# Scores of the first step issued early, its neighbour's loads moved to SyncE, and weight passes one by one, in a gated linear recurrence followed by a PReLU network

## The chip, the cores and the metric

The kernel runs on one core of one Trainium2 chip. A core has TensorE (PE, matmuls), VectorE (DVE), ScalarE (ACT), GpSimd (POOL) and SyncE (SP); the last two mostly issue transfers here. The metric is the device time of one execution in microseconds (us). The kernel before takes 625.14 us, the median of three executions (624.67, 625.14, 626.03).

## The reference

Two parts follow one another. The first is a gated linear recurrence over 768 tokens, for 4 batches, 8 heads and a head dimension of 48:

```python
f = 1.0 / (1.0 + np.exp(-f_logit))
for t in range(S):
    state = f[:, :, t, :, None] * state + np.einsum('bhd,bhe->bhde', k[:, :, t], v[:, :, t])
    y[:, :, t] = np.einsum('bhd,bhde->bhe', q[:, :, t], state)
```

Its output, regrouped to 3072 tokens of 384 numbers, goes through a feed-forward network with 2048 hidden units and a PReLU with one alpha per unit:

```python
h = x @ w_in                                        # 384 -> 2048
g = np.maximum(h, 0.0) + alpha * np.minimum(h, 0.0)
return (g @ w_out).astype(np.float32)               # 2048 -> 384
```

Inputs and output are float32. The weights reach the chip as 64-bit words that hold float64 values, and the kernel turns them into float32 itself.

## The kernel before

**Steps.** The sequence is cut into 6 chunks of 128 tokens, the batches into 2 pairs. A step is one chunk of one batch pair; the 12 steps run in the order (pair 0, chunk 0), (pair 1, chunk 0), (pair 0, chunk 1) and so on. Tiles of a step carry the suffix `pair_chunk`, so step 0 is `0_0` and step 1 is `1_0`. Each step passes through four generators:

- `prepare` (key P, or Q for the step to come) loads f, q, k and two halves of v, takes the sigmoid of f on ScalarE (L267), copies q into `qd` (L270), and forms on VectorE the products of decays that the scores need: `qd` with its four lags (L275), running products by two scans (L305, L307), `us` (from ScalarE's copies at L302, multiplied at L309), `k4` (L335), `kh`, `ks`, `q3` and, for chunk 0 alone, 16-column pieces `k16` and `q16` (L375, L392). At its end ScalarE copies `q3` into the matrix `A` (L407).
- `carry` (key O) multiplies the off-diagonal 32x32 blocks `off` (L432) and, for chunk 0, the 16-column blocks (L442). ScalarE copies the latter into `ad` (L446) and the former into `A` (L450). For chunk 0 it transposes `ks` on TensorE (`pk`, L459) and copies it to `ksn` (L462). Then the state products `pd` (L472) update the state kept in `vs` (L482 to L488).
- `attend` (key S) computes, for each batch u of the pair, the scores inside groups of four tokens (`raw`, 32 small matmuls for each u, L508), which VectorE merges into `ad` by four masked copies (L514), and the scores between groups (`qu`, L523), merged by three masked copies in chunk 0 (L545) and seven in the others (L529). ScalarE then copies `ad` into the diagonal blocks of `A` (L551), TensorE multiplies `A` with the state and values (`py`, L562), ScalarE copies the result to `y` (L571), and `xT`, the network's input, is made from `y`: in step 0 by matmuls (`xt`, L580, copied at L582), in the other steps by transfers.
- `network` (key n) computes eight blocks `ph` of the hidden layer, six matmuls each (L606); for each, ScalarE forms the negated negative part (`neg`, L611) and VectorE the gate (L613). Step 0 then multiplies by `w_out` plainly (`po`, L626). The other steps use a seven-product scheme (`pa` to `pe`, L645) on sums `S` of the gates (L687) and on sums of halves of `w_out` (L706, key W), which VectorE forms once.

**Weights.** `load_weights` brings each of `w_in` and `w_out` in 8 pieces of 767 KB into tiles `raw` on SP's queue (L196; four buffers, so the first four are issued at the start). For each piece ScalarE makes three passes: `pos` (L201), `neg` (L203) and `low` (L204), the last straight into the weight tile and the last reader of the `raw` tile; VectorE then forms `lead` from pos and neg (L214) and adds it into the weight tile (`both`, L219). One `a` (w_in) or `b` (w_out) in the order runs all three passes of one piece; `w` and `v` run one lead and the both of the piece before.

**Order.** The order on TensorE, VectorE and ScalarE is written out by hand; the two issuing engines follow by dependences. For step n the string `first[n]` (n from 0 to 3) or `usual` is read key by key; each key runs a generator up to its next `yield`, a number repeats it. In body n, key P, O and S belong to step n, n to the network of step n - 1, and Q to `prepare` of step n + 1.

**PSUM.** Two tiles of two banks (`pair`) serve off, pk, pd, raw, qu and py; four single banks (`bank`) serve ph, xt, po, pa to pe. At the start 56 tiny matmuls into the bank `idle` (L733) run before any other work of TensorE.

**Who loads.** Step 0's f, q, k and v are issued by SP ahead of the weights; all later steps' by POOL (L250).

Of the kernel before, what the change touches and what calls it, by code (L numbers as in the profile page):

```python
# [18 lines left out]
DB = 32  # L19
# [7 lines left out]
IDLE = 56  # L27
RAWS, TOPS, LEADS = 4, 3, 4
# [3 lines left out]
def kernel(  # L32
# [135 lines left out]
    def load_weights(dst, src, name):  # L168
# [17 lines left out]
        got = {}  # L186
# [7 lines left out]
        def upper(n):  # L194
            raw = stage.tile([128, WP, 4], I16, tag="raw", name=f"{name}_raw{n}", bufs=RAWS)
# [3 lines left out]
            top = raw[:, :, 2]  # L199
            pos = stage.tile([128, WP], I16, tag="pos", name=f"{name}_pos{n}", bufs=TOPS)  # L200
            nc.scalar.activation(pos, top, AF.Relu, bias=bias[:, 0:1], scale=8.0)  # L201
            neg = stage.tile([128, WP], I16, tag="wneg", name=f"{name}_neg{n}", bufs=TOPS)
            nc.scalar.activation(neg, top.bitcast(U16), AF.Relu, bias=bias[:, 1:2], scale=8.0)  # L203
            nc.scalar.activation(as_int(n, I32), by_row(raw.bitcast(U32)[:, :, 0]), AF.Copy, scale=2.0 ** -13)  # L204
            got[n] = raw, pos, neg
# [5 lines left out]
        def lead(n):  # L211
            raw, pos, neg = got.pop(n)
# [7 lines left out]

        def uppers():
            for n in range(pieces_):
                upper(n)
                yield
# [9 lines left out]
        return uppers(), rests()  # L234
# [11 lines left out]
    def prepare(bp, c, x):  # L246
# [3 lines left out]
        loads = nc.gpsimd if bp or c else nc.sync  # L250
# [169 lines left out]
    def carry(bp, c, x):  # L420
# [3 lines left out]
        off = pair(f"off_{i}")  # L424
        for u in range(U):
            for hp in range(HP):
                for cc in range(NC2):
                    g = (u * HP + hp) * NC2 + cc
                    o = (u * HP + hp) * DB
                    for par in range(2):  # L430
                        r_ = rows(par)
                        nc.tensor.matmul(off[CH * cc:CH * cc + DB, par, o:o + DB],  # L432
                                         lhsT=kh[r_, g], rhs=q3[r_, g, 2], start=True, stop=True)
        if not c:
            for u in range(U):
                for hp in range(HP):
                    for j in range(NJ):
                        g = (u * HP + hp) * NJ + j
                        o = U * HP * DB + (u * HP + hp) * 16
                        for par in range(2):  # L440
                            r_ = rows(par)
                            nc.tensor.matmul(off[DB * j:DB * (j + 1), par, o:o + 16], lhsT=x["k16"][r_, g],  # L442
                                             rhs=x["q16"][r_, g], start=True, stop=True)
            for u in range(U):
                o = U * HP * DB + u * HP * 16
                nc.scalar.copy(ad[:, u, :, :, 16:DB], off[:, :, o:o + HP * 16].rearrange("p r (h t) -> p r h t", h=HP))  # L446
        for cc in range(NC2):
            s_ = slice(CH * cc, CH * cc + DB)
            for par in range(2):
                nc.scalar.copy(A[s_, :, par * HP:(par + 1) * HP, CH * cc + DB:CH * (cc + 1)],  # L450
                               off[s_, par, 0:U * HP * DB].rearrange("p (u h t) -> p u h t", u=U, h=HP))
# [347 lines left out]
```

## Time and profile before

| What | us |
|---|---|
| Median of three executions | 625.14 |
| The profiled execution, whole | 626.43 |
| Its span (first to last instruction) | 624.6 |
| TensorE busy in the span | 589.2 (94%) |
| VectorE busy | 503.4 (81%) |
| ScalarE busy | 260.5 (42%) |
| POOL busy | 62.9 (10%) |
| First `ph` matmul of step 0 | starts 57.88 |
| Step 1's `f` lands; its sigmoid starts | 24.0; 36.55 |
| Last add of the first seven-product network | ends 158.3 |

A profile is of one execution. "Busy" is the time in which an engine executed something; matmul ends are modelled, so a busy TensorE need not be at its best. In a timeline a line reads: start, duration of the group, engine, source line, operation, output<-input by tile names, shape, number of instructions (a float32 matmul of the kernel shows as two), and in brackets the idle time before it with the engine, tile and line that ended it. "PEclk" and "granted clock" are the share of TensorE's full clock that it was given. Line numbers are those of the kernel before.

### The profile page before, as it was taken

The page shows a single profiled execution, that of the slowest core. Times are in us where ns is not written, and L with a number is a line of the kernel's source. Part 1 is how long each engine was busy: PE and PEld are TensorE (multiplying, and loading weights), DVE is VectorE, ACT ScalarE, POOL GpSimd, SP SyncE. Part 2 cuts the span into 40 slices and gives each one's busy share as a digit, 9 for nine tenths or more (in the row PEclk, how much of TensorE's full clock was granted, in tenths as well). Part 3 has the DMA queues.
Part 4 walks back from the last instruction along what each step waited for, and adds up shares of the span by engine and source line. Part 5 has one row for each costly group of instructions (what it writes and reads, how often), then busy time and mean ns, then how long its engine had stood idle before and what let it go on. Part 6 is the DMA issues. An engine that isn't in the chain of part 4 may idle for free.

```text
span 624.6 us, 19118 instructions
## 1 busy us (share of the span) xinstructions
PE 589.2 (94%) x8220; PEld 525.9 (84%) x8220; DVE 503.4 (81%) x1013; ACT 260.5 (42%) x482; POOL 62.9 (10%) x119
## 2 busy tenths in 40 slices
PE   3457999999999999999999999999999999999997
PEld 3346876789889889889889889889889889889997
DVE  7589989899799798889889888888888889762261
ACT  5797992261443252342343343243244244223110
POOL 9120010001001001001001001001001000000000
PEclk9998999899999999999999999999999999999999
DMA  9866513213314313413413313413314301201000
GB/s 298 278 225 196 200 41 93 75 35 86 87 36 90 82 35 86 87 35 85 87 35 85 75 49 85 83 38 87 73 49 85 68 22 26 53 3 26 26 0 26
DMA packets 68116, 50.43 MB, mean 81 GB/s; under 512 B 47168, under 2 KB 60608, under 8 KB 68032
## 3 DMA queue, kind: packets, MB, share of 16 engines
q1 hardware_dynamic: 56656, 25.01, 15.8%
q0 software_dynamic: 6864, 22.35, 12.6%
q10 hardware_dynamic: 4512, 1.85, 1.6%
q8 instruction: 65, 1.06, 0.8%
q14 instruction: 19, 0.16, 0.1%
HBM read 36.21 MB, written 4.72 MB: 66 GB/s over the span
## 4 chain that ended last, share of the span: by engine, by line
PE 60%; DVE 18%; ACT 16%; issue 4%; DMA 1%; ACTq 1%; DVEq 0%
PE ph L606 24%; PE pc L645 9%; PE pa L645 6%; PE pe L645 5%; PE pd L645 5%; ACT A L551 4%; ACT us L302 3%; DVE gate L613 3%; PE qu L523 3%; DVE S L687 3%; PE raw L508 3%; DVE qd L275 2%; PE py L562 2%; ACT neg L611 2%; PE pb L645 1%
## 5 line engine op out<-in xcount | busy, mean ns | idle before, releaser
L606 PE MATMUL ph<-xT,w_in_sb 128*128 128x256 f32 x1152 | 262.7, 385 | 0.0
L606 PEld LDWEIGHTS ph<-xT,w_in_sb 128*128 128x128 f32 x1152 | 216.8, 191 | 33.1 <-issue 2.6
L611 ACT ACTIVATE neg<-ph 128x512 f32<-128x512 f32 x96 | 57.1, 596 | 197.2 <-PE ph L606 156.1
L613 DVE SCALAR_TENSOR_TENSOR gate<-neg,om,ph 128x256 f32<-128x256 f32 x192 | 82.2, 478 | 50.3 <-ACT neg L611 50.2
L645 PE MATMUL pc<-t,S 128*128 128x192 f32 x352 | 61.7, 329 | 0.0
L645 PE MATMUL pa<-w_out_sb,gate 128*128 128x192 f32 x352 | 61.0, 327 | 0.0
L645 PEld LDWEIGHTS pa<-w_out_sb,gate 128*128 128x128 f32 x352 | 58.0, 190 | 0.6
L645 PEld LDWEIGHTS pc<-t,S 128*128 128x128 f32 x352 | 57.3, 190 | 0.6
L514 DVE COPY_PREDICATED ad<-mraw,raw 128x256 f32<-128x256 int32 (+1 forms) x96 | 42.4, 441 | 8.3 <-PE raw L508 5.8
L529 DVE COPY_PREDICATED ad<-mquad,qu 128x224 f32<-128x224 int32 (+6 forms) x140 | 41.9, 300 | 6.2
L407 ACT COPY A<-q 48x512 f32<-48x512 f32 x44 | 27.2, 617 | 37.4 <-DVE q L356 37.0
L551 ACT COPY A<-ad 32x256 f32<-32x256 f32 x96 | 38.6, 402 | 1.4
L318 DVE TENSOR_TENSOR us<-us,fs 128x768 f32<-128x768 f32 (+5 forms) x60 | 36.7, 612 | 0.0
L663 ACT COPY o<-pa 128x192 f32<-128x192 f32 x11 | 3.5, 318 | 75.3 <-PE pa L645 72.3
L562 PEld LDWEIGHTS py<-A,vs 128*64 128x64 f32 x768 | 25.7, 145 | 7.8 <-ACT A L551 3.3
L562 PE MATMUL py<-A,vs 128*64 128x64 f32 x768 | 28.7, 232 | 3.4 <-ACT A L551 1.4
L687 DVE TENSOR_TENSOR S<-gate 128x512 f32<-128x512 f32 x44 | 30.3, 688 | 0.8
L645 PE MATMUL pb<-t,gate 128*128 128x192 f32 x176 | 30.4, 326 | 0.0
L645 PE MATMUL pe<-w_out_sb,S 128*128 128x192 f32 x176 | 30.4, 326 | 0.0
L645 PE MATMUL pd<-w_out_sb,S 128*128 128x192 f32 x176 | 30.4, 326 | 0.0
L508 PEld LDWEIGHTS raw<-qd,k 48*32 48x32 f32 x1536 | 18.3, 109 | 14.0 <-issue 8.4
L508 PE MATMUL raw<-qd,k 48*32 48x80 f32 x1536 | 23.3, 243 | 6.8 <-ACT A L450 5.2
(109 smaller groups left out, 754.6 us busy)
## 6 DMA issues: line engine op xcount, KB each, us to landing
w_out_raw<-in_w_out SPq DMA_DIRECT2D x8, 767.8 KB, 4.4
w_in_raw<-in_w_in SPq DMA_DIRECT2D x8, 767.2 KB, 9.8
q<-in_qT POOLq DMA_DIRECT2D x11, 512.0 KB, 4.4
f<-in_fT POOLq DMA_DIRECT2D x11, 512.0 KB, 4.2
k<-in_kT POOLq DMA_DIRECT2D x11, 512.0 KB, 4.6
out<-o SPq DMA_DIRECT2D x24, 192.0 KB, 2.8
vs<-in_v POOLq DMA_DIRECT2D x22, 192.0 KB, 4.6
ksn<-kt SPq DMA_DIRECT2D x80, 32.0 KB, 2.0
```

The costliest lines, as they stand in the source:

```text
L318: nc.vector.tensor_tensor(us[:, :, UO[m]:UO[m] + 4 * n].rearrange("p g (i r) -> p g i r", r=4), us[:, :, skip:skip + 4 * n].rearrange("p g ...
L407: nc.scalar.copy(A[halves(cc)[1], :, par * HP:(par + 1) * HP, CH * cc:CH * (cc + 1)], q3[rows(par)].rearrange("p (u h c) s t -> p u h c (s ...
L508: nc.tensor.matmul(raw[DB * j:DB * (j + 1), par, hp * C:hp * C + QW], lhsT=k[r_, g * DB:(g + 1) * DB], rhs=qd[r_, g], start=True, stop=True)
L514: nc.vector.copy_predicated(adu[:, :, :, d:4], mraw[:, d, :, d:4].bitcast(I32).unsqueeze(1).broadcast_to((128, H, NB, n)), rv[:, :, QO[d]: ...
L529: nc.vector.copy_predicated(ad[:, u, :, :, 4 * m:DB], mquad[:, lo:lo + n].bitcast(I32).unsqueeze(1).unsqueeze(1).broadcast_to((128, 2, HP, ...
L551: nc.scalar.copy(A[s_, u, :, s_], ad[s_, u].rearrange("p r h t -> p (r h) t"))
L562: nc.tensor.matmul(py[64 * par:64 * par + 64, u, o:o + CH], lhsT=vs[bp][:, cc, u, hd * D:hd * D + 64], rhs=A[:, u, par * HP + hp, CH * cc: ...
L606: nc.tensor.matmul(ph[:, j * T:(j + 1) * T], lhsT=w_in_sb[:, kt, m * 128:(m + 1) * 128], rhs=xT[:, kt], start=(kt == 0 and j == 0), stop=( ...
L611: nc.scalar.activation(neg, phv, AF.Relu, scale=-1.0)
L613: nc.vector.scalar_tensor_tensor(gate[:, m % NH, m // NH], neg[:, j], om[:, m:m + 1], phv[:, j], ALU.mult, ALU.add)
L645: nc.tensor.matmul(to[:, 0:DH], lhsT=of(f), rhs=by(f), start=(f == 0 and not more), stop=(f == NH - 1), skip_group_check=True)
L687: nc.vector.tensor_tensor(to, x_, y_, op)
```

## The change

Six things change together.

1. The 56 tiny matmuls at the start become 46, and a new key J runs single filler matmuls (128x256) into the bank `idle`, later into a bank `spare`: 15 in all, inside step 0.
2. In step 0, `attend` issues the raw scores of both batches right after `qd` is ready, ahead of `off`, then merges both and issues both quad-score groups, then merges those. Later steps keep their order inside `attend`.
3. In step 0, `off` and `pk` take single banks instead of a pair. In all chunk-0 steps the 16-column blocks come before the 32-column ones, and their copy into `ad` is four instructions instead of two; step 0 yields between `off` and `pk`.
4. f, q, k and v of step 1 are loaded by SP instead of POOL. On SP's queue they stand behind six pieces of w_in.
5. One `a` runs one pass of one piece (pos, neg or low); one generator covers w_in and then w_out. Three `raw` buffers instead of four; piece n + 3 is requested after low of piece n.
6. The four strings `first` are rewritten; `usual` stays. In body 1, six blocks `ph` of step 0's network stand on TensorE ahead of off, pk and raw of step 1; before, off and pk stood ahead of all of them and raw behind the first ones.

The diff, cut to its core:

```diff
-IDLE = 56
-RAWS, TOPS, LEADS = 4, 3, 4
+IDLE = 46
+RAWS, TOPS, LEADS = 3, 3, 4
...
-        def upper(n):
-            raw = stage.tile([128, WP, 4], I16, tag="raw", name=f"{name}_raw{n}", bufs=RAWS)
+        def fetch(n):
+            raw = raws[n] = stage.tile([128, WP, 4], I16, tag="raw", name=f"{name}_raw{n}", bufs=RAWS)
             nc.sync.dma_start(...)
+        def upper(n):
             pos = ...
             nc.scalar.activation(pos, top, AF.Relu, bias=bias[:, 0:1], scale=8.0)
+            yield
             neg = ...
             nc.scalar.activation(neg, top.bitcast(U16), AF.Relu, bias=bias[:, 1:2], scale=8.0)
-            nc.scalar.activation(as_int(n, I32), by_row(raw.bitcast(U32)[:, :, 0]), AF.Copy, scale=2.0 ** -13)
+            yield
+            low = raws.pop(n).bitcast(U32)[:, :, 0]
+            nc.scalar.activation(as_int(n, I32), by_row(low), AF.Copy, scale=2.0 ** -13)
...
-        loads = nc.gpsimd if bp or c else nc.sync
+        loads = nc.gpsimd if c else nc.sync
...
-        off = pair(f"off_{i}")
+        def two(name):
+            if plain:
+                return [bank(f"{name}{n}_{i}") for n in range(2)]
+            t = pair(f"{name}_{i}")
+            return [t[:, n] for n in range(2)]
+        off = two("off")
...
             for u in range(U):
-                o = U * HP * DB + u * HP * 16
-                nc.scalar.copy(ad[:, u, :, :, 16:DB], off[:, :, o:o + HP * 16].rearrange(...))
+                for par in range(2):
+                    o = U * HP * DB + u * HP * 16
+                    nc.scalar.copy(ad[:, u, par, :, 16:DB], off[par][:, o:o + HP * 16].rearrange(...))
...
+        if (bp, c) == steps[0]:
+            raws = [scores(u) for u in range(U)]
+            yield
+            qus = []
+            for u in range(U):
+                within(u, raws[u])
+                qus.append(quad_scores(u))
+            yield
+            for u in range(U):
+                between(u, qus[u])
+            yield
+        else:
+            for u in range(U):
+                within(u, scores(u))
+                between(u, quad_scores(u))
+                yield
...
+    def kept_busy():
+        while True:
+            if not spare:
+                spare.append(bank("spare"))
+            nc.tensor.matmul(spare[0][:, 0:256], lhsT=ones[:, 0:128], rhs=ones[:, 0:256], start=True, stop=True)
+            yield
...
-        "P5 a w P a2 O w S w a w a2 S Q S O S w Q2 S Q2 S w",
-        "a2 w b w O w n2 b2 v S P v2 n2 S b v Q n b n O S2 v n b v n Q2 b v Q b n S v2 W Q W S n2 W n W",
-        "n S P n2 S n W n O Q n3 O S Q n S Q n Q S2 Q n3",
-        "S n3 P S Q S n O n O n4 Q S Q S Q n S Q n Q n2",
+        "J4 P J P a2 P a J a S J2 a J a2 J w a P J a2 P J3 w J O P S2 Q w a w a S O S O Q S a Q S a2 Q a2 w Q w",
+        "a2 n a2 w a2 n2 a n a w a P v a n w n O a3 S a2 v a n a S v a v S a n a2 v O a Q a4 n S v a4 Q v n a S n S v2 Q2 W n Q W3",
+        "n S n P n3 S Q S n2 O n O n S W n Q3 S2 Q n Q n2",
+        "S n2 S2 n Q n O Q n S n2 O n2 Q2 n S Q n2 S Q n",
...
+    def uppers(parts):
+        for n in range(RAWS):
+            parts[n][0](parts[n][2])
+        for n, (_, upper, m) in enumerate(parts):
+            yield from upper(m)
+            if n + RAWS < len(parts):
+                fetch, _, ahead = parts[n + RAWS]
+                fetch(ahead)
+            yield
```

## The prediction

> **What bounds the kernel now.** I read the page's totals and 40 slices first, then the waits of VectorE, then the timelines of TensorE and ScalarE at the places that the change touches, and the DMA issues last.
>
> ```profile
> PE 589.2 (94%) x8220; PEld 525.9 (84%) x8220; DVE 503.4 (81%) x1013; ACT 260.5 (42%) x482; POOL 62.9 (10%) x119
> ...
> PE   3457999999999999999999999999999999999997
> ...
> DVE  7589989899799798889889888888888889762261
> ACT  5797992261443252342343343243244244223110
> ```
>
> TensorE is full from slice 5 on; the first four slices (62 us) are all that a start-up change can shorten. But VectorE is above nine tenths in many slices until the tenth as well. Its waits between 12 and 160 us, by what released it (total, times, longest):
>
> ```profile
> DVE ad L514 <- PE raw L508: 4.8, 1, 4.8
> DVE gate L613 <- ACT neg L611: 4.3, 4, 1.3
> DVE w_in_lead L214 <- ACT w_in_neg L203: 2.4, 1, 2.4
> DVE w_out_lead L214 <- ACT w_out_neg L203: 1.0, 1, 1.0
> DVE qd L275 <- ACT qd L270: 0.6, 1, 0.6
> DVE us L309 <- ACT us L302: 0.5, 1, 0.5
> ```
>
> That is 13.6 us, the last of it before 91 us; from there to the end of the first seven-product network (the L672 add, ending 158.3 us) VectorE waits for nobody. So up to 158 us I keep the account by VectorE: its instructions number 1013 in both kernels, and the handover to a full TensorE moves by the change in the sum of these waits. The lines that carry the steps, TensorE first:
>
> ```profile
> 27.93 1.34 PE L508 MATMUL raw<-qd,k 48*32 48x80 f32 x64 [5.21 <-ACT A L450]
> ...
> 46.97 2.83 PE L580 MATMUL xt<-y,dense 128*128 128x256 f32 x12 [1.79 <-ACT y L571]
> ...
> 57.88 4.40 PE L606 MATMUL ph<-xT,w_in_sb 128*128 128x256 f32 x18
> ```
> ```profile
> 118.17 1.07 PE L523 MATMUL qu<-us,k 48*32 48x112 f32 x64 [1.19 <-DVE ad L529]
> 119.17 7.40 PE L606 MATMUL ph<-xT,w_in_sb 128*128 128x256 f32 x24
> ```
> ```profile
> 36.55 1.04 ACT L267 ACTIVATE f<-f 128x1024 f32<-128x1024 f32 x1
> ...
> 43.47 2.14 ACT L302 COPY us<-qd 128x256 f32<-128x256 f32 x4
> ```
> ```profile
> w_in_raw<-in_w_in SPq DMA_DIRECT2D x8, 767.2 KB, 9.8
> ...
> f<-in_fT SPq DMA_DIRECT2D x1, 512.0 KB, 4.0
> ...
> f<-in_fT POOLq DMA_DIRECT2D x1, 512.0 KB, 8.7
> ```
>
> To see: step 0's raw scores wait for the off-diagonal block; its network starts at 57.9; after a wait of 1.2 us among small matmuls, 24 first-layer instructions (two blocks) took 7.40 us where the same 24 take 5.45 at 110.68 (granted clock 0.77 over that stretch); and step 1's sigmoid starts at 36.6 although its f landed at 24.0.
>
> **The change part by part.** The sum is made against the profiled execution, 626.43 us (span 624.6, 1.8 around it); the median shown, 625.14, lies 1.29 under it, so a difference found on the profile is added to 625.14.
>
> *Early scores.* qd is ready at 10.6; the raw matmuls of both batches (64 instructions and 1.34 each) now run there, to 13.3. Their merge (L514) can't follow at once: VectorE first does step 0's products, which end at 20.2, and one lead pass is put in front of them that waits for neg0 (15.2 instead of 14.7: +0.5 wait, 0.5 work that is done anyway). So products end near 20.8, a lead and a both (1.5) follow, and the merges start at 22 instead of 29.42, behind the L446 copies (off 16-wide matmuls 1.43, copies 0.7). Waits of 2.4 and 4.8 go; the second quad-score pair comes 0.5 late. Two merges with quads (2 x 2.9) end near 28.5 instead of 38.1. L446 grows from 2 copies (0.41 together) to 4 (about 0.7): +0.3 on ScalarE in a stretch where it waits for f next, hidden.
>
> *Weights pass by pass, three buffers, and the loads on SP.* ScalarE's 4.0 us wait before L407 goes; passes run from 13.34 at 0.89, 0.87 and 0.79 each, so low0, low1 and low2 end at 16.0, 18.6 and 21.2. They release raw3, raw4, raw5 on SP, in order, and only behind raw5 stand f, q, k and two vs of step 1. f is issued at 21.2 + 0.65 = 21.9 (POOL issued it at 15.26). Bounds of its landing: 4.0 after issue, the row of an f on SP with nothing in front (25.9), and 8.7, the row of the crowded f (30.6). In front of it stand raw4 and raw5 partly, 1.0 to 1.5 MB at 376 to 417 KB per us (the full slices of the DMA view up to 45 us) 2.5 to 4 us, so I take 5.5 in all: 27.4. ScalarE reaches the sigmoid near 25.3 and waits 2.1; nothing else is behind it that VectorE could use except neg3. q and k land by about 31; q (ready about 29) is needed after kr at 29.1. POOL loses four of its DMA issues (2.8 us), none of which anyone waited on; the k row that POOL could issue only at 33.84, after the last raw score, lands 11 us sooner, with no reader before L335. Queued behind f on SP: q, k, vs (0.7 each), then raw6, which waits for low3 (31.8; before issued at 26.44), raw7 and the w_out pieces; raw6 lands at 31.8 + 4.4 and is read at about 46, so these waits are SP's alone; with three buffers instead of four the cover is 10 us, and a piece that came late would cost 2.6 us of passes.
>
> The Trainium skill, "DMA: Bandwidth & Descriptors", section "Issuing engines are not separate DMA queues", says that the issuing engines share the same 16 DMA engines, which speaks against any gain from changing the queue by itself. The trace agrees as far as it goes, raw4 taking 10.3 us to land beside POOL's loads; by the page alone f would be neutral, while by the issue times above it is later by the wait for low2.
>
> *ScalarE after f.* Sigmoid, kr, qd (2.74) end at 30.1; then neg3, low3 (1.7), A from ad (1.65), ksn (1.07), A (1.65), vs (0.96), and the us copies (2.14 + 0.3) end at 39.5. VectorE waits for qd (1.0 instead of 0.6) and, with its products, two leads and boths and scans done by 37, for us: 39.5 is 6.1 us earlier than 45.65 but a wait of 1.8 instead of 0.5.
>
> *TensorE.* y follows at 41 to 42, xt (2.8) and the first network block at about 45 to 47 instead of 57.88. The new order puts six blocks (6 x 2.65 = 15.9) ahead of step 1's off, pk and raw, which before stood in front. Off (1.5), the ad copies, off, A, pk, two ksn copies with ScalarE waiting about 1.1 three times, come to 5.8 us; so step 1's raw scores start near 67 instead of 63.51. VectorE, with the gates of six blocks (12 x 0.44) and the weight passes done by 62.7 to 63, waits there: 4.5 us until 67.5. This is where the start-up gain goes. Fillers: 15 at about 0.45 (a sixth of a block), all in waits of TensorE before 20 us, in a bank of their own: nothing; without that cover 6.8.
>
> *The account.* New waits: lead 0.5, quad 0.5, qd 1.0, us 1.8, gates and passes of the first network 1.0 + 1.3 + 1.6 (against 1.2 + 0.9 before), step 1's raw 4.5, gates 1.1, kr and qd of step 2 0.5 + 1.0, three short ones 0.4: 15.2 against 13.6: **+1.6 us** at the handover. After it the work is the same and TensorE full. For the half-clock stretch I assume one on TensorE's path in both kernels: before at 120.0 to 123.4, now probably near 155, after a wait for the c bank that u3 (L667) frees. None more costs -2.0 (7.40 - 5.45), one more +2.0. Nothing in between is known, so I take equal. 625.14 + 1.6 = 626.7.
>
> The Trainium skill, "TensorE: Matmul & The Clock Gate", section "The HAM clock gate", has the clock halve after an idle window of 3.4 us. Here it halved at 120.0 after only 1.2 us without any matmul, so by the page the new short waits would cost no clock (sum unchanged, or 2.0 less), by the row they may.
>
> **The rivals.** (1) *Faster: TensorE, not VectorE, is the bound between 100 and 158.* For it: it is 58.8 of 60 us busy there. Against: its own wait is for VectorE's L529. Then the network's start counts: 57.88 to 46 is 11.9 earlier, less off and pk moved behind it (4.5), less new waits of TensorE up to 108 (off 0.8, pk 0.9, pd 0.8, py 0.5, quad 1.6): -2.8, 622.3. VectorE's account gives the same (1.6 - 4.5 = -2.9) where the weight passes cover all of its wait for step 1's raw. It decides once VectorE's waits total under 12.3 us. (2) *Same: the two sums cancel within 1.25 us* (0.2%, about what a measurement of this kernel can tell from no change): the waits total 12.4 to 14.9, as with f at 26.3 and the rest as above: 625.5. (3) *Slower still: f, or the clock.* Every us that f lands later moves sigmoid, us, y and the network alike: 30.6 gives +3.2 more; and if the clock is low when xt and the first blocks start (its first warm stretch now ends in scattered small tiles), 2.8 to 5.5 us of work doubles for up to one 3.4 us stretch, +1.7: 628.5 to 631.5. (4) *It doesn't do what it says:* the merge still starts at 29, since ad is first written by L446. Then 4.8 stays and all follows 6 us later: above 631. Against: off needs only VectorE's products at 20.8.
>
> **How the numbers follow.** The likeliest, slightly slower: 0.37, own range 626.4 to 628.2. Rival 1: 0.29. Rival 2: 0.18. Rivals 3 and 4: 0.16. Faster 0.29, same 0.18, slower 0.53. The low end is rival 1 with f at 25.9 (622.3 - 1.5 = 620.8); the high end is rival 3 without its last 1.5 us, 630.0. Outside remain about 0.08 below and 0.07 above.
>
> **What would show it.** Right: raw at 10.6; the first merge at 22; f landing at 26 to 29 with ScalarE waiting for it; first network block at 45 to 47; VectorE waiting 4 us or more for step 1's raw near 63 to 67; the weight-half sums (L706, before at 105.4) at about 107; a row of 7.4 us for two blocks in one place only. Wrong: VectorE's waits up to 160 us below 13 us, or TensorE waiting for VectorE less than 3 us between 100 and 160; f landing past 29.5; a half-clock stretch at 42 to 50.

## The result, and the profile after

The changed kernel takes 632.12 us (median of 4; 630.77 to 633.46) against 624.96 us for the kernel before on the same chip: a ratio of 1.0112 with a 95% interval of 1.0096 to 1.0128. It is 7 us slower, where the prediction said 1.6 us slower with a range up to 630.0. The sign was right, the size was not, and the range did not hold it. The profiled execution is the 633.46 us one, with a span of 631.7.

The page's totals and three of its rows in 40 slices:

```profile
PE 601.0 (95%) x8230; PEld 533.6 (84%) x8230; DVE 504.4 (80%) x1013; ACT 261.9 (41%) x486; POOL 59.4 (9%) x114
...
PE   8569799989899999999999999999999999999997
...
DVE  7788489999899778889889888888889889762251
...
PEclk9759699999899999999999999999999999999999
```

VectorE is busy as long as before (504.4 against 503.4 us) with the same 1013 instructions. TensorE is busy 11.8 us longer: the fillers and tiny matmuls make 8.5 of it (9.5 and 5.1 us, where the kernel before has 6.1 of tiny ones), `xt` 1.9 (4.71 against 2.83) and `ph` 1.4 (264.1 against 262.7). On record, TensorE had half its clock in three stretches: 22.5 to 46.4, 66.8 to 77.1 and 162.4 to 165.8 us (the PEclk row shows the first two). The kernel before has low stretches of 3.4 us at 55.2 and at 120.0, and 1.00 ahead of them. But that early 1.00 can't be taken at its word: 60 matmuls `py` took 3.37 us there at 41.8, much as the 3.47 us of the changed kernel at 0.50, while run 7 below has 1.97 us at 1.00. So a low clock in the first 42 us is not shown to be new; that it lasted through `xt` is.

Line numbers from here on are those of each run's own kernel; in the changed one the gate is L649 (before L613), raw L519 (L508), qu L540 (L523) and ph L642 (L606). VectorE's waits between 12 and 160 us, in the same view as before the change (total, times, longest):

```profile
DVE gate L649 <- ACT neg L647: 5.9, 4, 2.9
DVE ad L528 <- PE raw L519: 5.3, 1, 5.3
DVE ad L565 <- PE qu L540: 2.1, 1, 2.1
DVE us L308 <- ACT us L301: 1.9, 1, 1.9
DVE qd L274 <- ACT qd L269: 1.8, 2, 1.0
DVE kr L277 <- ACT f L266: 0.4, 1, 0.4
DVE w_in_lead L218 <- ACT w_in_neg L205: 0.3, 1, 0.3
DVE w_out_lead L218 <- ACT w_out_neg L205: 0.2, 1, 0.2
```

These are 17.9 us, where the kernel before has 13.6: 4.3 more. The last add of the first seven-product network starts at 162.6 instead of 158.0: 4.6 later. The account that the prediction kept by VectorE's waits accounts for this part, and the difference lies in its terms.

TensorE's timeline in the first 80 us (start, duration, then the group; idle time before it and its releaser in brackets):

```profile
12.44 1.59 PE L519 MATMUL raw<-qd,k 48*32 48x80 f32 x128
...
23.86 0.76 PE L540 MATMUL qu<-us,k 48*32 48x52 f32 x36 [1.36 <-DVE ad L528]
26.87 1.43 PE L540 MATMUL qu<-us,k 48*32 48x52 f32 x92 [2.26 <-issue]
...
42.55 4.71 PE L616 MATMUL xt<-y,dense 128*128 128x256 f32 x12 [1.32 <-ACT y L607]
47.09 15.70 PE L642 MATMUL ph<-xT,w_in_sb 128*128 128x256 f32 x72
62.73 1.26 PE L440 MATMUL off<-us 48*32 48x16 f32 x128
64.66 0.76 PE L453 MATMUL off<-q,kh 48*32 48x32 f32 x64 [0.67 <-ACT ad L445]
65.34 0.66 PE L472 MATMUL pk<-ident,ks 128*128 128x128 f32 x4
68.83 1.01 PE L472 MATMUL pk<-ident,ks 128*128 128x128 f32 x4 [2.83 <-issue]
69.77 1.34 PE L519 MATMUL raw<-qd,k 48*32 48x80 f32 x64
...
72.97 4.87 PE L642 MATMUL ph<-xT,w_in_sb 128*128 128x256 f32 x12
```

Step 0's raw scores run at 12.4 instead of 27.9, and the network starts at 47.1 instead of 57.9. Then six blocks pass, and step 1's raw scores start at 69.8, where before they started at 63.5. Two things made step 1 late there: the second half of `pk` stood for 2.8 us on "issue" (it waited for nothing that the profile shows), and the clock was low from 66.8 on, so that the block behind step 1's first scores took 4.87 us instead of 2.7. At the end of the first seven-product network and later, two more waits stand in TensorE's timeline, the first before two blocks of which 3.4 us ran at the half clock, the second in the state products of a later step. In run 7 below, with the same orders, the same two blocks follow the same wait at the full clock. The three rows are the first wait, the same place in run 7, and the second wait:

```profile
162.04 7.13 PE L642 MATMUL ph<-xT,w_in_sb 128*128 128x256 f32 x24 [1.50 <-DVE Csum L703]
```
```profile
163.51 5.45 PE L642 MATMUL ph<-xT,w_in_sb 128*128 128x256 f32 x24 [1.50 <-DVE Csum L703]
```
```profile
225.60 0.92 PE L483 MATMUL pd<-vs,ksn 64*48 64x48 f32 x58 [1.28 <-DMA ksn<-kt]
```

From that add to the last one of its kind the kernel before takes 463.4 us (158.0 to 621.4) and this one 465.6 (162.6 to 628.2). So of 6.8 us, 4.6 lie ahead of the first such add and 2.2 behind it.

### The profile page after: what moved, and what is told of

It reads as the page before. It is cut to its first block, busy times and chain, and to the rows that moved or that the text cites. A ratio compares the mean times of both kernels' runs of the same rounds, so it can differ in the third digit from the quotient of the medians.

```text
span 631.7 us, 19137 instructions
## 1 busy us (share of the span) xinstructions
PE 601.0 (95%) x8230; PEld 533.6 (84%) x8230; DVE 504.4 (80%) x1013; ACT 261.9 (41%) x486; POOL 59.4 (9%) x114
## 4 chain that ended last, share of the span: by engine, by line
PE 62%; DVE 17%; ACT 8%; DMA 5%; SPq 3%; issue 3%; ACTq 0%; DVEq 0%
PE ph L642 24%; PE pc L681 8%; PE pa L681 6%; PE pd L681 4%; PE pe L681 4%; PE po L662 3%; PE py L598 3%; DVE gate L649 3%; DVE S L723 3%; SPq L414 3%; ACT A L587 3%; PE qu L540 2%; PE raw L519 2%; PE pb L681 2%; DVE qd L274 2%
## 5 line engine op out<-in xcount | busy, mean ns | idle before, releaser
L642 PE MATMUL ph<-xT,w_in_sb 128*128 128x256 f32 x1152 | 264.1, 387 | 3.0 <-DVE Csum L703 1.5
L642 PEld LDWEIGHTS ph<-xT,w_in_sb 128*128 128x128 f32 x1152 | 218.1, 192 | 36.8 <-issue 2.6
L649 DVE SCALAR_TENSOR_TENSOR gate<-neg,om,ph 128x256 f32<-128x256 f32 x192 | 82.5, 482 | 51.6 <-ACT neg L647 51.1
L406 ACT COPY A<-q 48x512 f32<-48x512 f32 x44 | 27.2, 617 | 39.5 <-DVE q L355 36.2
L274 DVE TENSOR_TENSOR qd<-qd,f 128x768 f32<-128x768 f32 (+2 forms) x36 | 27.8, 772 | 4.5 <-ACT qd L269 4.5
L540 PE MATMUL qu<-us,k 48*32 48x112 f32 (+1 forms) x1536 | 27.0, 262 | 4.5 <-issue 3.0
```

The lines of the kernel that those rows point to most:

```text
L274: nc.vector.tensor_tensor(qdv[d], qdv[d - 1][:, :, :, 1:5 - d], f[:, :, 1:5 - d].rearrange("p (g i) r -> p g i r", i=NB), ALU.mult)
L540: nc.tensor.matmul(qu[DB * j:DB * (j + 1), par, hp * QS + 4:hp * QS + QL], lhsT=k4[r_, g * DB:(g + 1) * DB], rhs=us[r_, g, 4:QL], start=Tr ...
L642: nc.tensor.matmul(ph[:, j * T:(j + 1) * T], lhsT=w_in_sb[:, kt, m * 128:(m + 1) * 128], rhs=xT[:, kt], start=(kt == 0 and j == 0), stop=( ...
L649: nc.vector.scalar_tensor_tensor(gate[:, m % NH, m // NH], neg[:, j], om[:, m:m + 1], phv[:, j], ALU.mult, ALU.add)
```

## The experiments

The first theory (A) was that the loss is VectorE's 5.3 us wait for step 1's raw scores, made by the order of body 1; its rivals, that f behind the weight pieces moves everything (B), or that the low clock up to 46 us does (C). The first four runs tell these apart, and the theory did not survive them as it stood.

**1. Loads by POOL again.**

```diff
-        loads = nc.gpsimd if c else nc.sync
+        loads = nc.gpsimd if bp or c else nc.sync
```

> The changed kernel with the second step's inputs loaded by POOL again; all else as changed. Theory A (the order of body 1 makes VectorE wait 5.3 us for the second step's raw scores; f is not on the path that sets the end): f lands earlier and ScalarE's 2.6 us wait for it shrinks, but the score wait stays within 1 us of 5.3; 630.5 to 632.5 us. Rival B (f behind six weight pieces moves everything behind it one to one): 628.5 to 630 us, with the network's first block 2 to 3 us earlier.

Measured: 635.3 us, 629.26 to 636.6, ratio 1.0151 [1.0099, 1.0202]. Both ranges of time are missed. The score wait stayed (5.5 us), as A said. B is neither supported nor ruled out: in the profiled execution, the slowest of the four, TensorE stood still inside step 0's 16-column blocks, VectorE's merges waited 6.1 us for ScalarE's copies of them, and step 1's sigmoid came at 32.1 instead of 27.7, with no wait for f:

```profile
27.23 0.43 PE L440 MATMUL off<-us 48*32 48x16 f32 x28 [6.33 <-issue]
```

**2. Step 1's off and scores sooner in body 1.** The order, changed up to its first scores (the rest is as in the changed kernel; in the trace the scores stand behind four and five network blocks, where the expectation has three and four):

```diff
-"a2 n a2 w a2 n2 a n a w a P v a n w n O a3 S a2 v a n a S v a v S a n a2 v O a Q ..."
+"a2 n a2 w a2 n O n a n S a w a P v a n S w n a5 v a n a v a v S a n a2 v O a Q ..."
```

> The changed kernel with one change in the order of body 1: off and pk of the second step stand behind two blocks of the first network instead of six, its raw scores behind three and four. Theory A: the score wait of 5.3 us falls below 1.5 us, the low clock between 66.8 and 77.1 goes, VectorE's waits up to 165 us fall from 17.9 to 12 to 14, time 625 to 628 us. Rival B (late f) and rival C (the loss is in TensorE's low clock up to 46 us): less than 1.5 us gained, 630.6 to 632.5 us.

Measured: 635.5 us (633.7 to 636.88), ratio 1.0171 [1.0145, 1.0197]: slower than the changed kernel. The score wait did go, as theory A said, but another took its place. TensorE's timeline and VectorE's longest wait:

```profile
58.19 1.08 PE L453 MATMUL off<-q,kh 48*32 48x32 f32 x64 [4.06 <-ACT ad L445]
```
```profile
DVE gate L649 <- ACT neg L647: 13.7, 6, 7.9
```

The 32-column blocks now wait for ScalarE's copies of the 16-column ones, and those stand in ScalarE's order behind weight passes; the next network blocks stand behind the 32-column ones.

**3. Old orders of bodies 2 and 3.** In the changed kernel, `first[2]` and `first[3]` are those of the kernel before.

> The changed kernel with the orders of bodies 2 and 3 of the kernel before; bodies 0 and 1 as changed. Theory A: the waits up to 105 us stay; the 1.3 us wait of the state products for their transposed keys at 225 us goes, and the 1.5 us wait with the half clock at 162 us may go; 628.5 to 631 us. If the whole loss came from bodies 0 and 1, no change: 631.5 to 632.5 us.

Measured: 634.44 us (632.87 to 634.65), ratio 1.0150 [1.0125, 1.0174]: no gain. The wait at 225 us and that at 162 us are gone, but in this profile VectorE waited 20.3 us, with stalls of TensorE of 3.9 and 2.8 us on "issue" inside step 0's off and qu.

**4. Old orders of bodies 1 to 3.** Also `first[1]` is that of the kernel before, one old `a` or `b` written as three of the new `a`.

```diff
-"a2 n a2 w a2 n2 a n a w a P v a n w n O a3 S a2 v ..."
+"a7 w a3 w O w n2 a6 v S P v2 n2 S a3 v Q n a3 n O S2 v n a3 v n Q2 a3 v Q a3 n S v2 W Q W S n2 W n W"
```

> The changed kernel with the orders of bodies 1 to 3 of the kernel before (its weight passes in threes, as there), so that of the order only body 0 is changed. Theory A: the loss is made by body 1 and later, so 623 to 627 us, with the first network block later than 47 us but no 5 us score wait. Rivals B and C (the loss is made in body 0, by f or by the clock): 629 to 632 us.

Measured: 633.48 us (631.35 to 634.22), ratio 1.0135 [1.0111, 1.0159]. Theory A falls in this form: with the old orders the loss is as large. The wait is where run 2 had it, only longer:

```profile
51.96 1.47 PE L440 MATMUL off<-us 48*32 48x16 f32 x128 [4.16 <-DVE us L391]
60.97 1.08 PE L453 MATMUL off<-q,kh 48*32 48x32 f32 x64 [7.54 <-ACT ad L445]
```

So the second set of theories: D, the new form of `carry` in step 1 makes TensorE wait for ScalarE; E, the loss is made in body 0, where TensorE runs out of instructions and its clock is low.

**5. Old carry in step 1.** Step 0 keeps its form; for step 1 the 32-column blocks come first, the 16-column ones next, then all copies, and both halves of pk ahead of both copies.

```diff
+        if not plain:
+            wide()                  # the 32-column matmuls
         if not c:
             ...                     # the 16-column matmuls, their copies into ad
+        if plain:
+            wide()
...
+                if plain:
+                    nc.scalar.copy(ksn[:, u], pk[u])
+            if not plain:
+                for u in range(U):
+                    nc.scalar.copy(ksn[:, u], pk[u])
```

> The changed kernel, but for the second step the off-diagonal blocks go as before the change: 32-column blocks, then 16-column ones, then all copies by ScalarE; both halves of pk, then both copies. Step 0 keeps the new form. Theory D (in the second step TensorE now waits inside off and pk for ScalarE's copies of the same tile, 0.7 to 1 us each and more where ScalarE is in weight passes): off to first raw score takes 4 to 5 us instead of 7.0, 628.5 to 631 us. Theory E (the loss is made in body 0, where TensorE runs out of instructions under the weight loads and its clock is low to 46 us): no change beyond 1 us, 631 to 634 us.

Measured: 632.75 us, 627.43 to 634.06, ratio 1.0110 [1.0062, 1.0158]: no gain over the changed kernel that the interval would tell. The way from off to raw stayed 7.1 us (64.92 to 72.04), with 3.78 us of "issue" inside pk, so its profile can't show what the carry alone would save there.

**6. Old carry in step 1 and old orders of bodies 1 to 3.** Runs 4 and 5 together; only body 0, its fillers, its early scores, its loads and the one-by-one passes are new.

> The orders of bodies 1 to 3 of the kernel before, and the second step's off and pk as before; only body 0 and the loads are as changed. Theory D: the wait of 7.5 us of the 32-column blocks for ScalarE goes, the first network block starts at 55 to 58 us instead of 65, and the time is 623.5 to 627 us. Theory E: the first network block may come earlier, but at least 3 us of loss stay: above 628 us.

Measured: 624.77 us (10 runs, 623.72 to 626.08), ratio 0.9993 [0.9981, 1.0004]. Theory D held: from run 4 to this, 8.7 us for the carry alone. Theory E fell as a bound: the new body 0, with its loads and passes, costs nothing by itself, and gains nothing. The network's first block starts at 54.5 instead of 57.9, but VectorE waits until 63.5 for its first gate (its waits between 12 and 160 us, the four largest):

```profile
DVE gate L660 <- ACT neg L658: 5.8, 2, 4.8
DVE us L308 <- ACT us L301: 1.9, 1, 1.9
DVE w_in_lead L218 <- ACT w_in_neg L205: 1.3, 2, 1.1
DVE kr L277 <- ACT f L266: 1.2, 1, 1.2
```

**7. and 8. More fillers, and none.**

```diff
-"... w a w a S O S O Q S a Q S a2 ..."
+"... w a w a S O S J5 O Q S J3 a Q S a2 ..."
```

> The changed kernel with eight more filler matmuls, five between pk and pd and three between py and xt of step 0. If the low clock between 22.5 and 46.4 us costs what xt shows (4.7 instead of 2.8 us): xt takes 2.8 to 3 us, the first network block starts 1.5 to 2.5 us earlier, the time is 629.5 to 631 us. If the start of the network is not on the path: 631 to 633 us.

Measured: 630.62 us (629.84 to 631.56), ratio 1.0093 [1.0074, 1.0112]. In the profile the clock is up again at 38.0 instead of 46.4, and xt took 2.83 us.

In run 8 the keys J are left out of `first[0]`.

> The changed kernel without its 15 fillers. If the fillers only fill waits of TensorE: within 1 us of 632. If the instructions that they take bring the stalls of 2 to 6 us inside the small matmuls of step 0 (theory E), the place of the stalls moves and the time changes by 2 us or more, down to 628 us. If the fillers hold the clock up for off and the quad scores of step 0: 0.5 to 1.5 us slower.

Measured: 629.97 us, 626.88 to 631.69, ratio 1.0091 [1.0066, 1.0116]. Both intervals overlap that of the changed kernel, so neither difference (-1.5 and -2.2 us in the medians) is told from none. Without fillers the early raw scores of both batches took 2.40 us instead of 1.59, while xt took 2.83 us, as before the change. The stalls moved: 3.1 us inside the 32-column blocks and 4.8 us inside the quad scores.

**9. In the kernel before: the loads alone.**

```diff
-        loads = nc.gpsimd if bp or c else nc.sync
+        loads = nc.gpsimd if c else nc.sync
```

> The kernel before with one part of the change alone: the second step's inputs loaded by SP behind six weight pieces. Its sigmoid starts at 36.6 us there, so if f lands before that (28 to 31 us) nothing moves: 624 to 626.5 us. If the weight pieces or the instructions suffer from the moved transfers: more than 627 us.

Measured: 625.58 us (10 runs), ratio 1.0004 [0.9994, 1.0013]. The moved loads by themselves cost nothing there.

**10. In the kernel before: the new carry alone**, in both chunk-0 steps.

```diff
+        # the 16-column matmuls, then:
+        for u in range(U):
+            for par in range(2):
+                nc.scalar.copy(ad[:, u, par, :, 16:DB], off[:, par, o:o + HP * 16]...)
+        # then the 32-column matmuls, and the copies into A
...
-            for u in range(U):
-                nc.scalar.copy(ksn[:, u], pk[:, u])
+                nc.scalar.copy(ksn[:, u], pk[:, u])    # inside the loop over u, after its transposes
```

> The kernel before with one part of the change alone: in both chunk-0 steps the 16-column blocks first, their four copies, then the 32-column blocks, and ksn copied half by half between the transposes. Theory F (each form that makes TensorE wait for ScalarE inside off costs what stands in front on ScalarE): in the second step the 32-column blocks wait for ScalarE's copies that run at 59.3 us, so the first network block starts at 62 to 64 us instead of 57.9 and VectorE's waits grow by 4 to 7 us: 629 to 633 us. If the new form only costs beside the new orders: within 1.5 us of before.

Measured: 633.7 us (633.51 to 634.34), ratio 1.0138 [1.0122, 1.0153]. One part of the change, alone, makes the kernel before 8.5 us slower, a little more than theory F's range allows. VectorE's waits grew from 13.6 to 21.9: by 3.0 for step 0's raw scores (7.8 against 4.8) and by 5.6 for the gates (9.9 against 4.3). TensorE's timeline shows it in step 0 and in step 1:

```profile
19.32 1.43 PE L433 MATMUL off<-us 48*32 48x16 f32 x128 [11.02 <-DVE us L392]
26.82 1.08 PE L446 MATMUL off<-q,kh 48*32 48x32 f32 x64 [6.06 <-ACT ad L438]
...
55.80 1.43 PE L433 MATMUL off<-us 48*32 48x16 f32 x128 [3.34 <-DVE us L392]
62.48 1.08 PE L446 MATMUL off<-q,kh 48*32 48x32 f32 x64 [5.25 <-ACT ad L438]
```

and ScalarE's shows what stood in front of the copies, here in step 1:

```profile
59.34 0.99 ACT L201 ACTIVATE w_out_pos<-w_out_raw,bias 128x768 int16<-128x768 int16 x1 [1.37 <-DVE w_in_lead L214]
60.24 0.97 ACT L203 ACTIVATE w_out_neg<-w_out_raw,bias 128x768 int16<-128x768 uint16 x1
61.11 0.89 ACT L204 ACTIVATE w_out_sb<-w_out_raw 128x768 int32<-128x768 uint32 x1
61.91 0.52 ACT L438 COPY ad<-off 128x64 f32<-128x64 f32 x4
```

In the old form TensorE goes on to pk and ph while the copies wait behind the passes; in the new form the 32-column blocks go into the tile that ScalarE still has to read, so TensorE waits with them.

**11. and 12. Towards a faster kernel.** Run 6 with another body 1: one network block ahead of off on TensorE, and ScalarE's copies of off and its negations ahead of the last weight passes of w_in and the first of w_out; run 12 has the fillers of run 7 besides.

```diff
-"a7 w a3 w O w n2 a6 v S P v2 n2 S a3 v Q ..."
+"a3 n a3 w O a w n w a3 S a3 v P a3 v2 n2 S a3 v Q ..."
```

> As the run with the old carry of the second step and the old bodies, but in body 1 one network block stands ahead of off on TensorE, and ScalarE copies off and forms the negated parts before the last six of its weight passes. By VectorE's account its 4.8 us wait for the first gate falls to 2 or less, the sum from 13.6 to 10 to 12 us: 621.5 to 624 us. If something else (TensorE, full from 55 us) holds the end: 624 to 626 us.

> The same with eight more fillers, five between pk and pd and three between py and xt of step 0: xt 1.9 us shorter; by VectorE's account 0.5 to 2 us less than without them, 620.5 to 623.5 us. If stalls of TensorE for instructions come with the fillers: slower by 2 us or more and with a wider spread.

Measured: 628.04 us (7 runs, 626.47 to 630.29), ratio 1.0045 [1.0028, 1.0063], and 625.84 us (12 runs, 624.25 to 627.68), ratio 1.0011 [0.9999, 1.0023]. Neither gained, and the first is slower than before by 0.3 to 0.6%. In the first, the wait for the first gate fell from 4.8 to 3.1 us, but VectorE's wait for step 1's f grew from 1.2 to 3.1 us and the sum was 14.5; in the second, TensorE stalled 6.4 us on "issue" before 60 us and VectorE waited 6.0 us for it in step 0.

**13. and 14. The new orders told apart.** Both with step 1's old carry: run 13 has the new body 1 and the old bodies 2 and 3; run 14 the old body 1 and the new bodies 2 and 3.

> The changed kernel with the second step's old carry and the old orders of bodies 2 and 3; of the orders bodies 0 and 1 are new. If body 1 makes the loss (six network blocks ahead of the second step's off): VectorE still waits 4 to 6 us for raw, 629 to 633 us. If bodies 2 and 3 make it: 624 to 626.5 us.

> The changed kernel with the second step's old carry and the old order of body 1; bodies 2 and 3 are new. If body 1 makes the loss: 624 to 627 us, more than 624.8 by what the new bodies 2 and 3 cost (the 1.5 us wait for the u3 sum, the 1.3 us wait for transposed keys). If bodies 2 and 3 make it: 629 to 633 us.

Measured: 632.43 us (632.07 to 633.13), ratio 1.0118 [1.0101, 1.0135], and 625.86 us (10 runs), ratio 1.0008 [0.9993, 1.0024]. With the old carry, body 1 makes the loss; what bodies 2 and 3 cost is not told from nothing here, though the 1.5 us wait for `Csum` is in run 14's profile. Which part of body 1 does it was not separated: run 2, which moved the scores alone, had the new carry.

**15. and 16. f ahead of the fourth weight piece on SP**, in run 12's kernel and in the changed kernel.

```diff
+    def fetch_f():                  # key F in first[0], behind the third P
+        t = early["1_0"] = work.tile([128, W], F32, tag="f", ...)
+        nc.sync.dma_start(out=t, in_=fT[...])
-"... J P a2 P a J a S ..."
+"... J P a2 P F a J a S ..."
```

> The kernel with old carry, one network block ahead, and eight more fillers, and besides it the second step's f issued by SP ahead of the fourth weight piece. If f is what eats the gain of the early scores: ScalarE's wait for f goes, VectorE's waits fall below 12 us, 621.5 to 624.5 us. If stalls of TensorE for instructions eat it: 625 to 627 us.

> The changed kernel with the second step's f issued by SP ahead of the fourth weight piece; all else as changed. Prediction's step (f moves all behind it one to one, 2.6 us of wait here): 629 to 630.5 us. If the second step's scores, behind six blocks, are the next thing that is late: 631 to 633 us.

Measured: 624.24 us (12 runs, 620.31 to 626.94), ratio 0.9982 [0.9962, 1.0003], and 630.76 us (8 runs, 626.92 to 634.28), ratio 1.0086 [1.0060, 1.0113]. In both, ScalarE's wait for f was gone. Run 15 is the fastest kernel of the study by its median and lies where its expectation put it if f had eaten the gain (waits of 9.2 us), but its interval still reaches no change. Its profiled execution (620.84 us) shows VectorE's waits when TensorE does not stall for long (1.4 us of "issue" before 60 us):

```profile
DVE gate L662 <- ACT neg L660: 2.9, 3, 1.3
DVE w_out_lead L218 <- ACT w_out_neg L205: 2.6, 2, 1.6
DVE us L310 <- ACT us L303: 1.9, 1, 1.9
DVE ad L578 <- PE qu L553: 1.3, 1, 1.3
DVE ad L562 <- PE ph L655: 0.5, 1, 0.5
```

**The account over all runs.** VectorE's waits between 12 and 160 us (the view summed), the start of the first seven-product network's last add, the difference of the two, and the time from that add to the last one of the kernel, each from the profiled execution:

| Kernel | Waits | That add | Difference | From there to the last |
|---|---|---|---|---|
| Before | 13.6 | 158.0 | 144.4 | 463.4 |
| Changed | 17.9 | 162.6 | 144.7 | 465.6 |
| 1 loads by POOL | 22.2 | 167.1 | 144.9 | 464.5 |
| 2 scores sooner | 22.3 | 167.4 | 145.1 | 462.4 |
| 3 old bodies 2, 3 | 20.3 | 165.0 | 144.7 | 464.1 |
| 4 old bodies 1 to 3 | 21.2 | 164.9 | 143.7 | 463.5 |
| 5 old carry | 19.9 | 164.7 | 144.8 | 464.2 |
| 6 old bodies and carry | 12.6 | 156.5 | 143.9 | 463.3 |
| 7 more fillers | 19.6 | 164.0 | 144.4 | 462.4 |
| 8 no fillers | 14.9 | 159.2 | 144.3 | 462.5 |
| 9 before, SP loads | 14.9 | 159.1 | 144.2 | 462.7 |
| 10 before, new carry | 21.9 | 166.0 | 144.1 | 462.8 |
| 11 sooner | 14.5 | 158.1 | 143.6 | 463.4 |
| 12 sooner, fillers | 13.2 | 157.1 | 143.9 | 463.6 |
| 13 old carry, new body 1 | 18.2 | 163.5 | 145.3 | 463.8 |
| 14 old carry, old body 1 | 14.4 | 158.6 | 144.2 | 462.6 |
| 15 run 12, f first | 9.2 | 152.6 | 143.4 | 463.0 |
| 16 changed, f first | 14.4 | 158.7 | 144.3 | 463.0 |

Waits range over 13 us; the difference stays within 143.4 to 145.3, and the last column within 462.4 to 465.6. The steady difference by itself says only that VectorE has the same work ahead of that add in every kernel; with the steady last column it says that the sum of VectorE's waits in the first 160 us moves the end one to one. It is the sum that counts: a wait that goes can come back at VectorE's next instruction, as below with f. The last column has its own cause. Of the kernels with the new bodies 2 and 3, those whose clock fell behind the wait for `Csum` (runs 1 and 5) have 464.5 and 464.2, and runs 2, 7, 8, 14 and 16, where it did not, 462.4 to 463.0.

**Carry and body 1 together.** Medians with the new body 0 throughout:

| | Step 1's old carry | New carry |
|---|---|---|
| Old orders of bodies 1 to 3 | 624.77 (run 6) | 633.48 (run 4) |
| New orders | 632.75 (run 5) | 632.12 (changed) |

Either of the two costs about 8 us, and both together no more than one. With the old orders the new carry puts TensorE behind ScalarE's weight passes. Run 13, with the old carry and only body 1 new, agrees (632.43). With the new orders ScalarE is past its passes when off comes (TensorE waits 0.7 us), and step 1's scores are late anyway, behind six network blocks: VectorE waits 5.1 to 5.4 us for them in the changed kernel and in runs 5 and 13.

## Why the prediction was wrong

**Right: what bounds the time.** "The handover to a full TensorE moves by the change in the sum of these waits" held in all 18 profiles as far as the handover. That the start-up gain would not reach the end, and where it would go (VectorE's wait for step 1's raw scores), held too: 4.5 us expected, 5.3 measured.

**Right: most of the chain.** The first network block at 45 to 47 us (47.1), a wait of 1.8 us for the us copies (1.9), the first merge at 22 (21.8), f landing with ScalarE waiting for it (27.7, a wait of 2.6, expected 27.4 and 2.1), the half-clock row after a wait for the u3 sum near 155 (162.0). That f came on time is luck: it was issued at 20.3 instead of 21.9 and took 7.4 us to land instead of 5.5.

**Wrong: the sum of VectorE's new waits, 15.2 instead of 17.9.** This is the step that failed first; the path was right and its terms were too small:
- From the lead to the us copies, "lead 0.5, quad 0.5, qd 1.0, us 1.8" make 3.8; 0, 2.1, 0.8 and 1.9 were measured, 4.8. The view puts 2.1 on the quad scores, where TensorE stalled 2.3 us on "issue" inside the first quad group. But the stall is not the price: VectorE's next work needs step 1's f and qd, and qd's first product started at 30.8. Run 13, with the same body 0 and no such stall, waited 0.4 for the quads but 1.5 for f's kr and 1.1 for qd, and started that product at 31.1. So the early merges only brought VectorE sooner to a wait for f.
- "Step 1's raw 4.5" measured 5.3, and the "5.8 us" from the end of the six blocks to raw measured 7.0, with 2.8 us of "issue" inside pk; runs 7 and 8, which have no stall there, waited 1.4 us at that place for ScalarE's copy. The view of the kernel before had such "issue" rows (2.8 us before pd, 1.4 inside off), and no term was made of them.
- "Gates 1.1" behind it measured 2.9: that block ran at the half clock. The prediction had allowed a low clock up to the network's first blocks, not behind step 1's off, pk and raw. Small matmuls and short waits stood ahead of the 120.0 us stretch before, too, and the same row could have been applied here.
- On the other side, "lead 0.5" measured nothing, since the first weight piece landed sooner (its pass started at 11.1, before at 13.3), and the gates and passes of step 0's network waited 3.1 instead of 3.9.

**Wrong: "I take equal" for the half-clock stretch.** Before, the low stretch at 120.0 lay under VectorE's work. It was not free there either: VectorE's only wait between 91 and 158, which the prediction overlooked when it let VectorE wait for nobody from 91 on, is for the slow block behind that stretch:

```profile
124.69 0.87 DVE L613 SCALAR_TENSOR_TENSOR gate<-neg,om,ph 128x256 f32<-128x256 f32 x2 [0.93 <-ACT neg L611]
```

So it cost 0.9 us there. At 162 it lay behind the handover, on TensorE's path. There it costs 1.7 us (7.13 against 5.45), and a wait of 1.3 us for transposed keys at 225 us, for which the prediction had no term, comes on top. The table bears this out: with the same bodies 2 and 3, runs 2, 7 and 8 have neither (run 7 waits 0.3 us for the keys) and 462.4 to 462.5 us in the last column; runs 1 and 5 have the stretch alone, and 464.5 and 464.2; the changed kernel has both, and 465.6. Against the kernel before (463.4) 2.2 us remain. The stretch is a chance and not a fixed price, since five of the eight profiles with that wait for `Csum` do not have it.

**Wrong: the carry as a detail.** The prediction priced the four copies at +0.3 "hidden" and ScalarE's three waits inside that chain as about 1.1 each, and had no term for TensorE waiting behind ScalarE's weight passes. Alone, that part costs 8.5 us in the kernel before (run 10, both chunk-0 steps) and 8.7 in step 1 alone with the old orders (runs 4 and 6). It did not make the miss of this kernel, where the wait is 0.7 us, but it is why putting the order right does not mend it (runs 2 and 4), and no experiment on order alone could be read without it.

**The rivals.** Rival 1 (TensorE bounds 100 to 158 us, 622.3) is out: in the changed kernel VectorE waited 0.5 us in all between 91 and 162 while TensorE's first block stood 10.8 us earlier than before. One sign named against VectorE's account did come, TensorE waiting less than 3 us for VectorE between 100 and 160 (2.5), so that sign was badly chosen; the 1.5 us for `Csum` follow just behind. Rival 2's sum (12.4 to 14.9) and rival 4's late merge did not come. Of rival 3, f landing late did not come, but the low clock did, through xt (+1.9) until 46.4, which the prediction had named as a sign of being wrong, and again from 66.8. Its f term is not told apart by the times of run 16, whose median is 1.4 us below the changed kernel's with intervals that overlap. In the profile of run 16, its fastest execution, it shows: the sigmoid starts 2.4 us sooner, the us copies, y and xt 2.05, and VectorE's waits up to the us copies are 2.8 instead of 4.8. There xt took 2.83 us instead of 4.71 as well, so the network started 3.9 us sooner; the waits fell by 3.5 and the add came 3.9 earlier.

**The clock rule.** The prediction set the rule of the Trainium skill's page "TensorE: Matmul & The Clock Gate", section "The HAM clock gate" (the clock halves after an idle window of about 3.4 us) beside the row at 120.0. The runs side with the row: the low stretch at 66.8 began 0.8 us into the pk stall, with 0.7 us of waiting in the 3.3 us of small matmuls ahead of that stall, and the one at 162.4 after a wait of 1.5 us. By that rule neither was to be expected. The row does not make a rule either: the same wait of 1.5 us left the clock at 1.00 in runs 2, 7, 8, 14 and 16 and was followed by the half clock in the changed kernel and in runs 1 and 5. What decides is not shown.

**What stays open.** What the "issue" stalls are. In three of them (24.6 to 26.9 in the changed kernel, 20.9 to 27.2 in run 1, 28.5 to 31.3 in run 3) one 16 KB packet of an instruction queue moved within the stall or from just ahead of it, in the first beside data transfers at 358 GB/s; that points to TensorE waiting for its own instructions, but no run separated it, and run 6 moved such packets at 22 and 29 us without a stall. Up to 60 us they vary from kernel to kernel with the same body 0 (none in runs 4 and 6, 6.7 us in run 3). Several kernels with the new body 0 also spread more from execution to execution (run 15 by 6.6 us over 12, run 16 by 7.4 over 8) than the kernel before does (3.1 us over 27), though run 6 does not (2.4 over 10). Since each account above is of one execution, part of the difference between two kernels can be such stalls.

## What to carry to other kernels

Find the engine whose waits set the handover and keep the account by its waits alone: here the sum of VectorE's waits in the first 160 us moved the end one to one, and 3 to 11 us gained on the start of TensorE's network (run 6 and the changed kernel) brought nothing by themselves. When a matmul writes into a tile that another engine must still read, the matmul inherits all that stands in that engine's queue; look there before regrouping copies. "Issue" waits and low-clock stretches that the old trace shows in small matmuls belong in the sum as terms, on the path or off it by place, and not only in the range.

## What the runs showed that was not expected

- The clock can be low while TensorE is at work: in the changed kernel it was 0.50 from 22.5 to 46.4 us, with TensorE busy 13.3 of 23.9 us, mostly in small matmuls, and xt took 4.71 us instead of 2.83. With eight fillers more between pk and xt it was up again at 38.0, but the time gained was not told from none.
- On record the clock is 1.00 until its first change, even where matmuls take as long as at 0.50 (`py` 3.37 us in the kernel before).
- TensorE stalled for up to 6.3 us (run 1) in the middle of a group of equal matmuls, with nothing to wait for in the profile; between 12 and 60 us the sum of such waits was from 0 to 8.3 us in kernels that do the same work.
- Moving 1.9 MB of loads from POOL to SP changed nothing by itself (run 9, 1.0004 with an interval of 0.9994 to 1.0013), with f, q, k and v behind six pieces of 767 KB.
